# Hash attention with a gated feed-forward layer: two more transposes of x handed to DMA, and means, hashes, loads and sends in other slots

## The chip, the cores and the metric

The kernel runs on one core of a Trainium2 chip. A core has five engines that run side by side, each through its own stream of instructions, in order: TensorE (PE; PEld in the profile is its loading of weights), VectorE (DVE), ScalarE (ACT), GpSimd (POOL) and SyncE (SP), which here only starts DMAs. They meet through semaphores. DMAs are started by SP, by POOL or by ACT, and 16 DMA engines carry them. The metric is the device time of one execution in microseconds; the median of three runs of the kernel before is 327.64 us (327.44 to 327.68).

## The reference

```python
q_bits = (np.einsum('bhsd,dk->bhsk', q, proj) > 0)      # 6 bits for each row, as a bucket number
k_bits = (np.einsum('bhsd,dk->bhsk', k, proj) > 0)
mask   = q_bucket[:, :, :, None] == k_bucket[:, :, None, :]
scores = np.where(mask, scale * np.matmul(q, k.transpose(0, 1, 3, 2)), -1e9)
attn   = softmax(scores)                                # with 1e-9 added to the sum
x      = np.matmul(attn, v)                             # heads side by side: (3072, 512)
xn     = x / sqrt(mean(x * x) + 1e-6) * rms_g
out    = (silu(xn @ w_gate) * (xn @ w_val)) @ w_out
```

There are 4 batches of 8 heads, 768 rows, 64 columns for each head; the feed-forward layer is 512 to 1536 to 512. All inputs and the output are fp32.

## The kernel before

**Units and slots.** The work is cut into eight units: unit u is one half (384 rows) of batch u // 2. Unit u's attention goes head by head, and a head takes three slots; there are 192 slots in the main loop (line 889). In slot t, TensorE first gets the two score matmuls of slot t + 1 (`scores`, L349), ACT the exponential of slot t (`probs`, L361), and then everything that the list `plan[t]` holds, in order of insertion. The order of every engine's stream is thus written out by hand through `at(0, t, function, ...)`; nothing is reordered later. From unit 2 on, unit u's attention runs in slots 24u to 24u + 23. In the same slots stand the second half of the layer before: y = h w_out of unit u - 2 (`project`, L513, with a copy and a store to memory for each third), and then gate and value matmuls of unit u - 1 (`gate`, `value`, L484).

**The planner.** `spread` (L805 to L828) lays a window's `project` pieces and gate and value pieces over its slots by weight, so that each slot carries about as much as the others. At given slots it puts in extras: `hash_one` (weight 1000) and `v_mean` (weight 120). An entry `(HASH, None)` takes up the weight of a hash and does nothing; it stands where a pair's hash is done together with the next pair's (`WITH`, L780).

**A pair of heads** (b, hp) is heads 2hp and 2hp + 1 of batch b. Q, K and V are loaded by SP (`load_natural`, `load_v`, `load_blocks`) into eight buffers that rotate. Q and K are transposed, for the first six pairs on TensorE (`turn_pe`, L156), later on VectorE (`turn_dve`, L188 and L195), and cast by GpSimd (`cast_pool`) to rows 0 to 63 of one of six fp16 tiles `QK`. The hash is a matmul with the projection (`hash_direct` L238, `hash_one` L218); VectorE turns its signs into fp16 bit rows (L227), and small DMAs (`send_bits`, L308: eight for a pair, four for a head) put them into rows 64 to 69 of `QK`. The score matmul then adds a large constant for each equal bit, and the exponential's bias takes it away again: unequal buckets come out as zero.

**Means.** `v_mean` (L333) sums V's rows through a matmul with ones; times 1e-9 / 768 the sum is added to the numerator and denominator of attention (`cvb`, L336), for the reference's 1e-9. For batch 0's later pairs it reads the fp16 V (`parts`), otherwise GpSimd's partial sums (`v_sum`). Batch b's two means of four heads are extras at 5 and 18 slots into the batch.

**From attention to the layer.** `attn_out` (L388 to L404) adds cvb, takes the reciprocal on VectorE, and multiplies on GpSimd (or on VectorE, with `eng`), which gives x. The squares' sums go to `ssp`; `norm` (L446) forms 1/rms on GpSimd (L443) and xn on VectorE, in thirds of 128 rows. Each third must be transposed to xnT: either by TensorE (`turn_x`, L467) with a copy out of PSUM by VectorE (L473), or by a DMA that SP issues (`turn_dma`, L431). `ONDMA` (L426) says how many thirds of a unit go by DMA; those are scaled by `grow` in xn (L452), the others by `gcol` in the copy. A unit's first gate matmul needs all three. `norm` stands 4 slots into the window, `turn_dma` 5.

**PSUM.** Transposes, hashes, means, gates, values and y share three banks (`bank`).

Of the kernel before, what the change touches and what calls it, by code (L numbers as in the profile page):

```python
# [16 lines left out]
H = 8  # L17
S = 768
D = 64
DMODEL = H * D  # L20
# [13 lines left out]
def kernel(  # L34
# [12 lines left out]
    nc = tc.nc  # L47
# [40 lines left out]
    raw = {}  # L88

    def load_natural(eng, b, hp, which, heads=(0, 1)):  # L90
# [10 lines left out]
            ),  # L101
        )

    def load_v(eng, b, hp):
        vn = lpool.tile([128, 2, 6, D], FP32, name="vn", tag="L")
        eng.dma_start(
            out=vn.rearrange("p h c d -> p h (c d)"),
            in_=v[b, 2 * hp : 2 * hp + 2].rearrange("h (p c) d -> p h (c d)", c=6),
        )
        raw[b, hp][2] = vn  # L110

    def load_blocks(eng, b, hp):
        tiles = []
        for name, t in (("qL", q), ("kL", k)):
# [8 lines left out]
            tiles.append(lt)  # L123
        raw[b, hp] = tiles + [None]

# [173 lines left out]
        for n, pair in enumerate(pairs):  # L299
            hashed[pair] = where, bt, 12 * n  # L300

    def send_bits(b, hp, hh):

        where, bt, r = hashed[b, hp]
        for t, which, half in where:
            o = (0 if which == "q" else S) + half * HALF
            p0 = 32 * t + r + 6 * hh
            nc.sync.dma_start(  # L308
                out=QK[b, 2 * hp + hh, "h"][D:KROWS, o : o + HALF],
                in_=bt[p0 : p0 + 6, :],  # L310
            )
# [5 lines left out]
        eng.tensor_copy(vls[b % 2][:, hs, :, 0:64], vn)  # L317

    def v_sum(b, hp):
        vn = raw[b, hp][2]  # L320
# [4 lines left out]
        nc.gpsimd.tensor_add(vsum[b % 2][:, hs, 0:64], a[:, :, 0], a[:, :, 2])  # L325

    def v_mean(b, hp, n, parts=(None,)):

        hs = slice(2 * hp, 2 * hp + n)
        ps = bank("m_ps", [128, n, 65])  # L330
        for i, jt in enumerate(parts):
            rhs = vsum[b % 2][:, hs, 0:65] if jt is None else vls[b % 2][:, hs, jt, 0:65]
            nc.tensor.matmul(  # L333
                ps, ones16, rhs, start=(i == 0), stop=(i == len(parts) - 1)
            )
        nc.vector.tensor_scalar_mul(cvb[b % 2][:, hs, 0:65], ps, C0 / S)  # L336
# [44 lines left out]

    def attn_out(u, hp, eng=nc.gpsimd):
        b = u // 2
        if hp == 0:
# [38 lines left out]

    rstds = {}

    ONDMA = {2: 2, 3: 2, 4: 2, 5: 2, 6: 2, 7: 1}  # L426

    def turn_dma(u, c):
        if c == 0:
# [168 lines left out]
    def at(w, s, f, *a):  # L598
        plan[NS * w + s].append(lambda: f(*a))
# [70 lines left out]
    at(0, 1, load_natural, nc.sync, 0, 3, "q")  # L670
    at(0, 2, load_v, nc.sync, 0, 2)
    at(0, 2, load_v, nc.sync, 0, 3)
    at(0, 60, nc.sync.dma_start, grow, moe_rms_g.partition_broadcast(128))
    at(0, 65, nc.scalar.mul, grow, grow, float(DMODEL) ** 0.5)
    at(0, 6, v_prep, 0, 1)
    at(0, 15, v_prep, 0, 2)
    at(0, 19, v_prep, 0, 3, nc.vector)
    for hp, t in enumerate((6, 16, 21, 28)):
        at(0, t, v_mean, 0, hp, 2, *([range(6)] if hp else []))
    for i, (t, t2) in enumerate(((22, 25), (31, 31))):  # L680
        cols = slice(i * DFF // 2, (i + 1) * DFF // 2)
# [2 lines left out]
        at(0, 39 + 3 * i, load_w, wo, moe_w_out, 6 * i, 6)  # L684


    for hp, ts in ((0, (8, 22, 23, 24, 25, 24, 39, 26, 28, 42)), (1, (20, 27, 28, 29, 30, 29, 41, 32, 33, 43))):
        tl, ts = ts[0], ts[1:]
        for w in "kq":
            at(0, tl, load_natural, nc.sync, 1, hp, w)  # L690
        at(0, tl, load_v, nc.sync, 1, hp)
        at(0, ts[0], new_pair, 1, hp)
        for t, hh, w in zip(ts[0:4], (0, 1, 0, 1), "kkqq"):
            at(0, t, turn_pe, 1, hp, hh, w)
        at(0, ts[4], cast_pool, 1, hp, "k")
# [7 lines left out]
    spots = {  # L703
# [10 lines left out]
    }  # L714
    for i, t in ((0, 39), (1, 41), (2, 57), (3, 61)):
        at(0, t, zero_rows, i)
    TX = 37

    LAGS = (0, 0, 0, 0, 0, 1, 1)
    sqs = {}  # L720

    def o_step(u, hp, *eng):
# [11 lines left out]
    late = []  # L734
    for n, (u, h) in enumerate(order):
        t = 3 * n + 4 - ((u, h) == (0, H - 1))
        for part in range(2):
            at(0, t + part, av, u, h, part)
        if h % 2:
            if (u, h) == (0, H - 1):  # L740

                at(0, t + 1, o_step, u, h // 2, nc.vector)
                at(0, t + 1, norm_scale, u)
                at(0, t + 1, nc.vector.tensor_scalar_mul, gcol, gcol, float(DMODEL) ** 0.5)
                at(0, t + 2, hash_only, 1, 1)
                at(0, t + 2, hash_signs, 1, 1)
                at(0, t + 2, norm, u)
                at(0, TX-1, norm_third, u, 2, nc.scalar.mul)
                at(0, TX + 1, send_pair, 1, 1)
                for c in range(3):  # L750
                    at(0, TX, turn_x, u, c, c == 2)
                continue
            if (u, h) == order[-1]:
                at(0, t + 1, o_step, u, h // 2, nc.vector)
                continue

            steps = [(t + 1, o_step), (t + (3 if h == 7 else 4 if u == 7 else 6), s_step)]
# [24 lines left out]
        spot[3]: (HASH, hash_one, *WITH.get(pair, ()), pair) for pair, spot in spots.items()  # L782
    }
    for (pair,) in WITH.values():
        inserts[spots[pair][3]] = (HASH, None)
    for b in (1, 2, 3):
        for s, hp in ((5, 0), (18, 2)):
            assert 2 * b * NS + s not in inserts
            inserts[2 * b * NS + s] = (MEAN, v_mean, b, hp, 4)


    SENDS = {(2, 0, 0): 77, (2, 0, 1): 77, (2, 2, 1): 101, (3, 2, 1): 149}

    def place(t, step):
        if step[0] is None:
            return
        at(0, t, *step)
        if step[0] is hash_one:
            late.append((t, hash_bits, *step[1:]))
            for pair in step[1:]:  # L800
                for hh in range(2):
                    s = SENDS.get((*pair, hh), t)
                    late.append((max(s, t), send_bits, *pair, hh))

    def spread(t0, n, pieces):  # L805
        fixed = [SCORES + (AV if (t - 1) % 3 < 2 else 0) for t in range(t0, t0 + n)]
# [3 lines left out]
        for s in range(n):  # L810
            done += fixed[s]
            while i < len(pieces):
                weight, whole, steps = pieces[i]
                full = done + weight // 2 > total * (s + 1) // n
                if extra and whole and t0 + s >= extra[0][0] and (full or extra[0][1] > MEAN):
                    _, weight, *step = extra.pop(0)
                    place(t0 + s, step)
                    done += weight
                    continue
# [45 lines left out]
    def behind_norm(t):  # L865

        return t - t % NS + 9 if 1 <= t % NS < 9 else t

    for (b, hp), (load, kturns, qturns, _) in spots.items():
        at(0, load, load_blocks, nc.sync, b, hp)  # L870
        at(0, load, load_v, nc.sync, b, hp)
        at(0, min(kturns + qturns), new_pair, b, hp)
        for w, turns in (("k", kturns), ("q", qturns)):
# [74 lines left out]
```

## Time and profile before

| | us |
|---|---|
| median of three runs (lowest, highest) | 327.64 (327.44, 327.68) |
| the profiled execution, its own time | 326.68 |
| its span, from the first instruction to the last | 324.9 |
| ACT: 192 exponentials of 128x768 (L361) | 167.7 busy, 900 ns each |
| PE: scores, 384 matmuls of 128x384 (L349) | 93.5 busy |
| PE: gates and values, 768 matmuls of 128x384 (L484) | 82.7 + 81.8 busy |
| PE: transposes of x, 52 matmuls of 128x128 (L467) | 4.7 busy, 219 ns each |
| DVE: copies of those out of PSUM (L473) | 7.4 busy, 11 times |
| SP: DMA transposes of x (L431) | 11 issues |
| TensorE's granted clock | 0.999 |

The clock is granted in full all the time. A line of a timeline has the start in us, the length, the engine, the kernel's line, the operation, what it writes and reads, and the shape; "x4" is a run of four instructions, and a bracket names the idle time before it and what ended that. Consecutive matmuls overlap: the next one starts long before the one ahead has ended. Times of slots: TensorE begins slot 21 at 27.64, slot 54 at 73.91, slot 119 at 177.81 and slot 148 at 222.44.

### The profile page before, as it was taken

The numbers are of one execution on the slowest core, as the hardware profiler recorded it, in microseconds if no ns is written. First come the engines' busy times: TensorE is split into PE (matmuls) and PEld (weight loads), VectorE is DVE, ScalarE is ACT, GpSimd is POOL, SyncE is SP. The second block draws the span as 40 slices with busy tenths as digits, with TensorE's granted clock in tenths as the row PEclk, the third lists the DMA queues.
The fourth block names the chain that finished last, engine by engine and source line by source line (L and its number), as shares of the span: only waits on it lengthen the run. The fifth ranks groups of instructions, "written<-read, shape, count | busy, mean of one in ns | idle before, by whom it ended". The sixth has DMA issues, their size and how long they took to land.

```text
span 324.9 us, 7772 instructions
## 1 busy us (share of the span) xinstructions
PE 319.9 (98%) x2955; PEld 194.4 (60%) x2955; DVE 229.7 (71%) x512; ACT 228.4 (70%) x333; POOL 157.6 (49%) x204
## 2 busy tenths in 40 slices
PE   8999999999999999999999999999999999999996
PEld 3676666656566565655566565655666556665554
DVE  5887876859888568874888568785677536673870
ACT  7999887667688676776767776777777768744322
POOL 4999759955974363731883621752582111221000
PEclk9999999999999999999999999999999999999999
DMA  7942999988428864055547056002100030003002
GB/s 208 360 168 85 226 216 195 192 159 151 103 38 158 157 136 88 6 94 156 89 100 145 35 125 120 7 5 66 72 4 3 1 99 34 0 2 105 10 2 97
DMA packets 85741, 32.63 MB, mean 100 GB/s; under 512 B 70908, under 2 KB 82632, under 8 KB 85704
## 3 DMA queue, kind: packets, MB, share of 16 engines
q1 hardware_dynamic: 81800, 27.35, 36.1%
q0 software_dynamic: 3680, 4.72, 8.5%
q8 instruction: 23, 0.38, 0.5%
q14 instruction: 14, 0.11, 0.1%
q10 hardware_dynamic: 224, 0.07, 0.1%
HBM read 28.58 MB, written 6.29 MB: 107 GB/s over the span
## 4 chain that ended last, share of the span: by engine, by line
PE 98%; ACT 1%; DVE 0%; issue 0%
PE s_ps L349 20%; PE g_ps L484 19%; PE v_ps L484 19%; PE y_ps L513 18%; PE o_ps L374 11%; PE d_ps L218 2%; PE t_ps L156 2%; PE d_ps L238 2%; PE z_ps L580 1%; PE x_ps L467 1%; PE y_ps L532 1%; PE m_ps L333 1%; ACT psb L361 1%; DVE kT L158 0%; PE s_ps L156 0%
## 5 line engine op out<-in xcount | busy, mean ns | idle before, releaser
L361 ACT ACTIVATE psb<-s_ps,ebias 128x768 f16<-128x768 f32 x192 | 167.7, 900 | 20.0 <-PE s_ps L349 19.2
L349 PE MATMUL s_ps<-QK 128*128 128x384 f16 (+1 forms) x384 | 93.5, 326 | 1.2 <-ACT psb L361 1.1
L492 ACT ACTIVATE t<-g_ps 128x384 f32<-128x384 f32 x96 | 47.2, 492 | 52.2 <-PE g_ps L484 50.5
L484 PE MATMUL g_ps<-xnT,wg 128*128 128x384 f16 x384 | 82.7, 326 | 0.0
L484 PE MATMUL v_ps<-xnT,wv 128*128 128x384 f16 x384 | 81.8, 326 | 0.0
L501 DVE SCALAR_TENSOR_TENSOR a<-t,g_ps 128x384 f32<-128x384 f32 x96 | 53.0, 552 | 28.9 <-ACT t L492 27.2
L395 POOL TENSOR_TENSOR x<-otmp,rcp 128x384 f32<-128x384 f32 x30 | 25.1, 837 | 96.2 <-DVE rcp L393 95.8
L513 PE MATMUL y_ps<-wo,ht 128*128 128x512 f16 x276 | 67.7, 379 | 0.0
L502 DVE SCALAR_TENSOR_TENSOR ht<-a,v_ps 128x384 f16<-128x384 f32 x96 | 53.2, 554 | 11.5 <-PE v_ps L484 3.6
L374 PEld LDWEIGHTS <-psb 128*128 128x128 f16 x1152 | 51.9, 97 | 15.7 <-issue 1.2
L374 PE MATMUL o_ps<-vl,psb 128*128 128x65 f16 x1152 | 55.8, 193 | 0.0
L349 PEld LDWEIGHTS <-QK 128*128 128x128 f16 (+1 forms) x384 | 34.8, 98 | 33.7 <-issue 7.9
L484 PEld LDWEIGHTS <-wg 128*128 128x128 f16 x384 | 35.2, 97 | 21.2
L484 PEld LDWEIGHTS <-wv 128*128 128x128 f16 x384 | 35.1, 97 | 20.8 <-issue 0.2
L513 PEld LDWEIGHTS <-ht 128*128 128x128 f16 x276 | 24.9, 98 | 23.0
L525 ACT COPY ysb<-y_ps 128x512 f32<-128x512 f32 x23 | 13.5, 587 | 15.8 <-PE y_ps L513 15.8
L388 DVE TENSOR_TENSOR otmp<-o_ps,cvb 128x390 f32<-128x390 f32 x32 | 17.8, 557 | 7.1 <-PE o_ps L374 7.1
L208 POOL CAST QK<-qT 64x768 f16<-64x768 f32 x20 | 16.5, 823 | 10.3 <-DVE qT L195 9.5
L401 POOL TENSOR_TENSOR sq<-x 128x384 f32<-128x384 f32 x24 | 19.9, 828 | 1.9
L208 POOL CAST QK<-kT 64x768 f16<-64x768 f32 x20 | 16.4, 822 | 5.2 <-DVE kT L195 3.1
L473 DVE TENSOR_TENSOR xnT<-x_ps,gcol 128x512 f16<-128x512 f16 x11 | 7.4, 688 | 15.1 <-PE x_ps L467 15.0
L195 DVE STREAM_TRANSPOSE kT<-kL 128x192 f32<-128x192 f32 x32 | 16.4, 516 | 0.0
(85 smaller groups left out, 274.9 us busy)
## 6 DMA issues: line engine op xcount, KB each, us to landing
vn<-in_v_dram SPq DMA_DIRECT2D x16, 384.0 KB
out_dram<-ysb SPq DMA_DIRECT2D x23, 256.0 KB
qL<-in_q_dram SPq DMA_DIRECT2D x40, 96.0 KB
kL<-in_k_dram SPq DMA_DIRECT2D x40, 96.0 KB
kn<-in_k_dram SPq DMA_DIRECT2D x5, 384.0 KB
qn<-in_q_dram SPq DMA_DIRECT2D x5, 384.0 KB
wg<-in_moe_w_gate_dram POOLq DMA_DIRECT2D x2, 768.0 KB, 9.4
wv<-in_moe_w_val_dram POOLq DMA_DIRECT2D x2, 768.0 KB, 11.7
```

The source lines that it names most:

```text
L208: nc.gpsimd.tensor_copy(QK[b, 2 * hp + hh, "h"][0:64, o : o + S], src[64 * hh : 64 * hh + 64, :])
L349: nc.tensor.matmul(ps[:, j, 0:HALF], QK[b, h, "h"][rows, S + jt * 128 : S + (jt + 1) * 128], QK[b, h, "h"][rows, half * HALF : (half + 1) ...
L361: nc.scalar.activation(psb[u, h][:, 2 * ch : 2 * ch + 2, :], sps.pop((u, i))[:, :, 0:HALF], AF.Exp, bias=ebias, scale=ESCALE,)
L374: nc.tensor.matmul(o[:, c, hh, 0:65], psb[u, h][:, jt, c * 128 : (c + 1) * 128], vls[b % 2][:, h, 2 * (jt % 3) + jt // 3 if b in PARITY el ...
L388: nc.vector.tensor_add(tmp[:, :, :, 0:65], o[:, :, :, 0:65], cvb[b % 2][:, 2 * hp : 2 * hp + 2, 0:65].unsqueeze(1).to_broadcast([128, 3, 2 ...
L395: eng.tensor_mul(xd.rearrange("p c (h d) -> p c h d", h=2), tmp[:, :, :, 0:64], r.to_broadcast([128, 3, 2, 64]),)
L401: eng.tensor_mul(sq, xd, xd)
L484: nc.tensor.matmul(ps, w[:, kt, fs], xnT[u][:, kt, :], start=(kt == 0), stop=(kt == 3))
L492: nc.scalar.activation(t, fbank[u, ft, "g_ps"], AF.Tanh, scale=0.5)
L501: nc.vector.scalar_tensor_tensor(out=a, in0=t, scalar=1.0, in1=g, op0=ALU.add, op1=ALU.mult)
L502: nc.vector.scalar_tensor_tensor(out=ht[u][:, ft, :], in0=a, scalar=0.5, in1=vv, op0=ALU.mult, op1=ALU.mult)
L513: nc.tensor.matmul(y, ht[u][:, ft, c * 128 : (c + 1) * 128], wo[:, ft, :], start=(ft == 0), stop=(ft == NF - 1),)
```

## The change

The edits, by what they move:

1. `ONDMA`: unit 1's first two thirds go by DMA instead of TensorE (all three went by TensorE), unit 5's all three (two did). The load of `grow` moves from slot 60 to 3, its scaling on ACT from 65 to 49.
2. Unit 5's last pair is multiplied and squared on VectorE (`XDVE`).
3. The loads of pair (2, 0) move from slot 50 to 53 (K first, then Q) and 54 (V), behind unit 1's transposes in SP's order. Pair (1, 2)'s eight bit sends, on SP in slot 51, are issued by GpSimd in slot 54; its V work on GpSimd moves from 54 to 57. Two zeroings of `QK` tiles by GpSimd move from 57 and 61 to 66 and 69.
4. The hash of pair (1, 0) moves from slot 26 to 27, and the first transpose of K of pair (1, 1) from 27 to 26; that K is loaded in slot 17 instead of 20. The mean of pair (0, 3) moves from 28 to 21.
5. In `spread` an extra is put in at the first whole piece once it is a slot late, even where the slot isn't full, and the empty entry of pair (3, 0) is gone. By the planner's own arithmetic this moves pieces in slots 96 to 119 only: the means of batch 2 come in slots 101 and 114 (before: 103 and 119), gates and values up to four pieces later than before in the middle, and slot 119 now carries four of them where it had none. Unit 4 first uses the second mean in slot 116.
6. Five late V loads are two DMAs, one for each head (`VSPLIT`).
7. Two assertions: a mean is put in ahead of its use, and after its sums.

```diff
+    VSPLIT = {(2, 3), (3, 0), (3, 1), (3, 2), (3, 3)}
     def load_v(eng, b, hp):
-        eng.dma_start(
-            out=vn.rearrange("p h c d -> p h (c d)"),
+        for hs in (slice(0, 1), slice(1, 2)) if (b, hp) in VSPLIT else (slice(0, 2),):
+            eng.dma_start(
+                out=vn[:, hs].rearrange("p h c d -> p h (c d)"),
...
-    def send_bits(b, hp, hh):
+    def send_bits(b, hp, hh, eng=nc.sync):
-            nc.sync.dma_start(
+            eng.dma_start(
...
-    ONDMA = {2: 2, 3: 2, 4: 2, 5: 2, 6: 2, 7: 1}
+    ONDMA = {1: 2, 2: 2, 3: 2, 4: 2, 5: 3, 6: 2, 7: 1}
...
-    at(0, 60, nc.sync.dma_start, grow, moe_rms_g.partition_broadcast(128))
-    at(0, 65, nc.scalar.mul, grow, grow, float(DMODEL) ** 0.5)
+    at(0, 3, nc.sync.dma_start, grow, moe_rms_g.partition_broadcast(128))
+    at(0, 49, nc.scalar.mul, grow, grow, float(DMODEL) ** 0.5)
-    for hp, t in enumerate((6, 16, 21, 28)):
+    for hp, t in enumerate((6, 16, 21, 21)):
         at(0, t, v_mean, 0, hp, 2, *([range(6)] if hp else []))
-    for hp, ts in ((0, (8, 22, 23, 24, 25, 24, 39, 26, 28, 42)), (1, (20, 27, 28, 29, 30, 29, 41, 32, 33, 43))):
+    for hp, ts in ((0, (8, 22, 23, 24, 25, 24, 39, 27, 28, 42)), (1, (20, 26, 28, 29, 30, 29, 41, 32, 33, 43))):
-            at(0, tl, load_natural, nc.sync, 1, hp, w)
+            at(0, 17 if (hp, w) == (1, "k") else tl, load_natural, nc.sync, 1, hp, w)
...
-        (2, 0): (50, (63, 64, 65, 66), (67, 69, 70, 71), 73),
+        (2, 0): ((53, 53, 54), (63, 64, 65, 66), (67, 69, 70, 71), 73),
-    for i, t in ((0, 39), (1, 41), (2, 57), (3, 61)):
+    for i, t in ((0, 39), (1, 41), (2, 66), (3, 69)):
         at(0, t, zero_rows, i)
+    XDVE = (5,)
-            if (u, h) == order[-1]:
+            if (u, h) == order[-1] or u in XDVE and h == H - 1:
                 at(0, t + 1, o_step, u, h // 2, nc.vector)
...
     for (pair,) in WITH.values():
-        inserts[spots[pair][3]] = (HASH, None)
+        if pair == (2, 0):
+            inserts[spots[pair][3]] = (HASH, None)
+        else:
+            del inserts[spots[pair][3]]
-    SENDS = {(2, 0, 0): 77, (2, 0, 1): 77, (2, 2, 1): 101, (3, 2, 1): 149}
+    SENDS = {(1, 2, 0): 54, (1, 2, 1): 54, (2, 0, 0): 77, (2, 0, 1): 77, (2, 2, 1): 101, (3, 2, 1): 149}
+    ONPOOL = {(1, 2, 0), (1, 2, 1)}
...
-                if extra and whole and t0 + s >= extra[0][0] and (full or extra[0][1] > MEAN):
+                due = extra and t0 + s - extra[0][0]
+                if extra and whole and due >= 0 and (full or due or extra[0][1] > MEAN):
...
-        t = 54 if (b, hp) == (1, 2) else behind_norm(qturns[-1] + 2)
+        t = 57 if (b, hp) == (1, 2) else behind_norm(qturns[-1] + 2)
         at(0, t, v_prep, b, hp)
```

More of the change, by code (lines that the diff above doesn't have):

```diff
@@ L102, in load_natural, with load_blocks @@
         )
+    VSPLIT = {(2, 3), (3, 0), (3, 1), (3, 2), (3, 3)}
     def load_v(eng, b, hp):
         vn = lpool.tile([128, 2, 6, D], FP32, name="vn", tag="L")
-        eng.dma_start(
-            out=vn.rearrange("p h c d -> p h (c d)"),
-            in_=v[b, 2 * hp : 2 * hp + 2].rearrange("h (p c) d -> p h (c d)", c=6),
-        )
+        for hs in (slice(0, 1), slice(1, 2)) if (b, hp) in VSPLIT else (slice(0, 2),):
+            eng.dma_start(
+                out=vn[:, hs].rearrange("p h c d -> p h (c d)"),
+                in_=v[b, 2 * hp : 2 * hp + 2][hs].rearrange("h (p c) d -> p h (c d)", c=6),
+            )
         raw[b, hp][2] = vn
-    def load_blocks(eng, b, hp):
-        tiles = []
-        for name, t in (("qL", q), ("kL", k)):
+    def load_blocks(eng, b, hp, only=(0, 1)):
+        tiles = raw.setdefault((b, hp), [None] * 3)
+        for n in only:
+            name, t = (("qL", q), ("kL", k))[n]
             lt = lpool.tile([128, 24, 32], FP32, name=name, tag="L")
@@ L122, in load_blocks @@
                     )
-            tiles.append(lt)
-        raw[b, hp] = tiles + [None]
+            tiles[n] = lt
     PARITY = (0, 1)
@@ L319, in v_sum @@
     def v_sum(b, hp):
+        sums.add((b, hp))
         vn = raw[b, hp][2]
@@ L325, in v_sum @@
         nc.gpsimd.tensor_add(vsum[b % 2][:, hs, 0:64], a[:, :, 0], a[:, :, 2])
+    means, sums = set(), set()
     def v_mean(b, hp, n, parts=(None,)):
+        for p in range(hp, hp + n // 2):
+            assert parts != (None,) or (b, p) in sums
+            means.add((b, p))
         hs = slice(2 * hp, 2 * hp + n)
@@ L383, in attn_out @@
         b = u // 2
+        assert (b, hp) in means
         if hp == 0:
@@ L802, in place @@
                     s = SENDS.get((*pair, hh), t)
-                    late.append((max(s, t), send_bits, *pair, hh))
+                    eng = nc.gpsimd if (*pair, hh) in ONPOOL else nc.sync
+                    late.append((max(s, t), send_bits, *pair, hh, eng))
     def spread(t0, n, pieces):
@@ L869 @@
     for (b, hp), (load, kturns, qturns, _) in spots.items():
-        at(0, load, load_blocks, nc.sync, b, hp)
+        if type(load) is tuple:
+            for t, only in zip(load, ((1,), (0,))):
+                at(0, t, load_blocks, nc.sync, b, hp, only)
+            load = load[2]
+        else:
+            at(0, load, load_blocks, nc.sync, b, hp)
         at(0, load, load_v, nc.sync, b, hp)
```

## The prediction

> **What bounds the kernel.** I read the page's busy shares first, then its chain, then what TensorE waited for, then the timelines around the edited slots.
>
> ```profile
> PE 319.9 (98%) x2955; PEld 194.4 (60%) x2955; DVE 229.7 (71%) x512; ACT 228.4 (70%) x333; POOL 157.6 (49%) x204
> ...
> PE 98%; ACT 1%; DVE 0%; issue 0%
> ```
>
> TensorE is nearly the whole chain; the other engines have 29% or more to spare. So an edit pays by what it takes off TensorE's instruction stream, or by a short stall between two matmuls, and costs what TensorE then waits for. "Busy" counts a matmul until its modelled end and hides short stalls, so I go by starts: in the timeline the distance from one group's start to the next is what a group costs.
>
> The profiled execution took 326.68 us (span 324.9, 1.78 around it), 0.96 below the median 327.64. I work out a difference on the profiled execution and subtract it from the median.
>
> **Unit 1: two thirds of x by DMA.** TensorE before unit 1's first gate (start, length, group):
>
> ```profile
> 75.09 0.39 PE L467 MATMUL x_ps<-ident,xn 128*128 128x128 f16 x4
> 75.32 1.03 PE L513 MATMUL y_ps<-wo,ht 128*128 128x512 f16 x4
> ...
> 76.78 0.74 PE L467 MATMUL x_ps<-ident,xn 128*128 128x128 f16 x8
> 77.36 0.49 PE L349 MATMUL s_ps<-QK 128*128 128x384 f16 x2
> ...
> 78.82 0.49 PE L484 MATMUL g_ps<-xnT,wg 128*128 128x384 f16 x2
> ```
>
> Four transposes cost 75.32 - 75.09 = 0.23; the later eight 0.58, of which 0.12 is a wait for the first copy out of PSUM. Two thirds go, one (0.23) stays: 0.81 - 0.23 = **0.58 off the path**, and the first gate would start at 78.24. Bounds: 0.46 (the wait stays) to 0.58. The trace has a rule to weigh here. The row of these transposes has 219 ns each, but their starts are 0.23 / 4 = 56 ns apart, and the pitch is what the next matmul waits for. The Trainium skill, page "TensorE: Matmul & The Clock Gate", Part 4, gives about 275 ns for such a transpose in a kernel; by that figure the twelve of both units would be an estimated 3.3 us. The starts here speak against it as a price on the path.
>
> What the DMAs must meet:
>
> ```profile
> 72.47 0.88 POOL L443 TENSOR_TENSOR rstd<-ss,mhalf 128x3 f32<-128x3 f32 x1 [1.71 <-DVE ss L439]
> 73.39 2.76 DVE L460 TENSOR_SCALAR xn<-x,rstd 128x512 f16<-128x512 f32 x3 [1.00 <-POOL rstd L443]
> ```
>
> The two thirds now use the L452 form (750 ns; 1.41 for a pair): ready at about 74.14 and 74.81. They are issued by SP. For what an issue and its data take I use unit 5, the same two DMAs in a quiet stretch (last columns: DMA share, GB/s):
>
> ```profile
> 224.35 2.55 SPq L431 DMA_TRANSPOSE xnT<-xn  x2
> ```
> ```profile
> 227.50:228.00 0.50, 0.50 (x4) 0.26 (x3) 0.00 (x0) 0.50 (x1) 0.00 (x0) 1.00 0.13 23
> 228.00:228.50 0.50, 0.50 (x6) 0.25 (x5) 0.00 (x0) 0.09 (x1) 0.00 (x0) 1.00 0.03 9
> ```
>
> An issue holds SP 1.28 us, and the second one's data end before 228.0, at most 2.4 after its issue at 225.63. So in unit 1: issues at 74.2 and 75.5, data in by 77.9, the gate at 78.24: no wait, but only 0.3 to spare. Of the eleven issues the longest took 2021 ns; such a one would make the gate wait 0.4. The DMA engines moved at a share of 1.04 from 72 to 73 us; those are earlier loads, issued by 70.6. The loads of pair (2,0) that SP issued from 70.72 are now behind the transposes.
>
> **What queues behind that wait on SP**: eight block loads of (2,0) (3.46 + 2.65 = 6.1 us before), a store, its v. They end about 6 us later, at 83; data ended some 3 us after the last issue (77.04, traffic over at 80), so 86. VectorE turns these blocks first in slot 63, at 88.6. Price 0, bound 0 to 0.5; K goes first, which fits.
>
> **Unit 5: the last third by DMA, last x by VectorE.**
>
> ```profile
> 228.72 0.39 PE L467 MATMUL x_ps<-ident,xn 128*128 128x128 f16 x4
> 228.95 1.03 PE L513 MATMUL y_ps<-wo,ht 128*128 128x512 f16 x4
> ...
> 230.13 0.81 PE L484 MATMUL g_ps<-xnT,wg 128*128 128x384 f16 x4
> ```
>
> **0.23 goes**; the gate would start at 229.90. The third DMA is issued at 226.9, its data end by 229.3: 0.6 to spare. VectorE's chain to xn: the multiply on GpSimd (837 ns, with a hop) becomes one of 558 on VectorE, but a stream transpose of 0.5 that ran beside GpSimd now stands behind the squares: equal within 0.1. Four bit sends and two stores come 1.3 later on SP; the bits are for unit 6's head 5 (slot 158, 237 us). Bounds 0 to 0.23.
>
> **The early slots.** A mean that stood in a stall, and one in slot 28; and the stall after the mean of slot 119:
>
> ```profile
> 27.97 0.51 PE L333 MATMUL m_ps<-vl,ones 128*128 128x130 f16 x6
> 28.43 0.48 PE L349 MATMUL s_ps<-QK 70*128 70x384 f16 x2
> ...
> 178.40 0.28 PE L333 MATMUL m_ps<-vsum,ones 128*128 128x260 f16 x1
> 178.69 0.48 PE L349 MATMUL s_ps<-QK 128*128 128x384 f16 x2
> ```
>
> Six mean matmuls take 0.35 in slot 28 (34.45 to 34.80) but 0.46 in slot 21: 0.11 is a wait of the scores for ACT's exponentials. Pair 3's mean moved there fills it: **0.11**. Its vl is ready at 26.73 (VectorE's cast). The hash of pair (1,0) costs 31.88 to 33.18 = 1.30 with its scores, against 1.23 at 23.86; VectorE's last Q copy ended at 32.36, after the hash had begun. One slot later it doesn't: **0.07**. Its K of (1,1) is needed a slot earlier and loaded three slots earlier, behind transposes done at 23.1: covered. Both are bounded by 0 and themselves, since ACT (8.93 us busy of the ten from 20 to 30) can take the slack back.
>
> **The planner, slots 96 to 119 (unit 4's attention).** With no empty 1000-weight entry for (3,0), slots 96 to 119 carry even work, and batch 2's second mean moves from 119 to 114. In 119 the mean took 0.29 to the next scores, against 0.12 at 73.79: slot 119 was 0.88 long and ACT's exponential takes 0.90. **0.17** goes, bounds 0 to 0.17. The mean in 114 (PE at 171) needs sums that GpSimd ended at 166.1: no wait.
>
> **Parts at nothing.** grow's load in slot 3 adds 256 KB ahead of the bits of (0,1); about 0.9 us at the page's 290 GB/s, and the bits, issued by 17.0 on SP, are used at 20.9. Its 639 ns on ACT move to slot 49, beside 1.10 of idle at 68.39. Zeroing moves 2 x 2.65 of GpSimd time to 95 and 101, where it idles 1.74 and 3.36. Five split v loads add 5 x 0.6 on SP; the tightest is (3,0), ahead of four sends and unit 3's transposes (149.53 to 149.95, with TensorE's gate at 154.13 and data by 153.7). All bounds 0 to 0.3.
>
> **Bits of (1,2) by GpSimd.** No row has a small DMA from this queue. The bounds: SP's eight sends took 5.75, 0.66 to 0.93 each; GpSimd's own weight loads
>
> ```profile
> L585 POOL DMA_DIRECT2D wg<-in_moe_w_gate_dram x2: 806/906/1007, 30.3 to 38.5; - x2
> ```
>
> took up to 1.01, with 8.9 us or more to landing for 768 KB. GpSimd is free for them at 73.35. Head 4's four are issued by 77.4 at the latest, and the scores that read them stand at 82.34 - 0.58 = 81.76. With SP's kind of landing (last of four issued at 80.0, read without a stall at 82.34) they are early; with 8.9 us they would be 4.5 late. I take 0: 4.5 KB is nearer to SP's row than 768 KB is. GpSimd is held for at most 8.1 us, so x of unit 2 starts 1.4 later than 80.06, and pair (1,3)'s casts end near 89.9 instead of 88.05, for scores at 91.3: covered by 1.4.
>
> **Sum**: 0.58 + 0.23 + 0.11 + 0.07 + 0.17 = 1.16. 326.68 - 1.16 = 325.5 for the profiled execution, and 327.64 - 1.16 = **326.5** for the median.
>
> **The rivals.**
> - *A gate waits for its DMA transposes* (17%). For: 0.3 and 0.6 to spare, an issue of 2021 ns in the rows. Against: none of the other units' gates waits on one now. It returns 0.4 to 0.9: 326.9 to 327.4.
> - *GpSimd's queue is late* (9%): slower. If its small DMAs land more than 8.4 us after 73.35 for four of them (1.4 each and 2.8 to land, say), TensorE stands at head 4's scores, 1 us for each us; over 1.2 us of GpSimd per send, the casts of (1,3) are late too. From 1.2 us of lateness the kernel is slower; at the 4.5 above it is 331. The Trainium skill, page "SBUF — State Buffer", section "SBUF: two separate sides", says that VectorE in a two-port mode keeps GpSimd from writing descriptors, so that a DMA of 620 ns took 3100; by it four sends would be an estimated 12 us. Against: in that stretch VectorE has one short row of such a form (480 ns), among rows that read PSUM or two tensors.
> - *Only the transposes pay* (8%): the early and planner terms are taken back by ACT: 327.64 - 0.81 = 326.8.
> - *A transpose costs its duration* (2%): 12 x 219 ns = 2.6, with the rest 324.7. Pitch speaks against it.
> - *More than the sum* (4%): GpSimd's and VectorE's relief around 75 us closes other short stalls: 326.0.
>
> **How the numbers follow.** The forecast has 60%, 326.1 to 326.9. The range 325.9 to 327.8 takes in the waiting gates and the lesser sums, and leaves out the late queue and the duration rival. About 0.2% (0.65 us, to 326.98) is what a measurement can tell from no change. Faster: 60 + 4 + 2 and half of the 8: 70%; within: the other half and the waiting gates but 1, 20%; slower: the late queue, and 1 from a gate that waits longest, 10%.
>
> **What would show it.** TensorE's x_ps group at 40 instead of 52 matmuls; unit 1's first gate right behind its y_ps group; no stall of the scores after the mean near 28 and near slot 119; GpSimd's eight issues each under 1.0 us, and no wait at head 4's scores near 81. A DMA named as releaser of g_ps or s_ps would prove me wrong, as would a GpSimd send of over 1.2 us.

## The result, and the profile after

The changed kernel takes 328.03 us (median of 22 runs, 327.60 to 328.92) against 327.28 for the kernel before on the same chip (22 runs, 326.73 to 328.26). The ratio is 1.0024, with a 95% interval of 1.0016 to 1.0031: slower by some 0.75 us, where 1.16 us of gain was predicted. The profiled execution took 328.73 us, span 326.9. Of the runs below, one execution of e5_shift took 670 us and one of e8_before_shift 415 us; they are in no ratio.

The page of the changed kernel, busy shares and the chain that ended last:

```profile
PE 320.4 (98%) x2943; PEld 194.0 (59%) x2943; DVE 227.5 (70%) x510; ACT 228.4 (70%) x333; POOL 160.4 (49%) x211
...
PE 94%; DMA 2%; DVE 1%; ACT 1%; SPq 0%; issue 0%; POOL 0%
```

The twelve transposes are gone from TensorE (2955 to 2943 matmuls), but the chain now leaves TensorE: 2% of the span is time in which it runs through a DMA, from issue to landing. (In the changed kernel L359 are the scores, L495 gates and values, L442 the DMA transposes, L312 the bit sends.) Its TensorE timeline shows where (start, length, group, and in a bracket the idle time and its releaser). The four places are the means in slot 21, which now take 0.69 for twelve, and the first gates of units 1, 3 and 5:

```profile
29.00 0.85 PE L343 MATMUL m_ps<-vl,ones 128*128 128x130 f16 x12
29.69 0.49 PE L359 MATMUL s_ps<-QK 70*128 70x384 f16 x2
...
78.21 1.02 PE L524 MATMUL y_ps<-wo,ht 128*128 128x512 f16 x4
79.51 0.48 PE L495 MATMUL g_ps<-xnT,wg 128*128 128x384 f16 x2 [0.27 <-DMA xnT<-xn]
...
153.94 1.03 PE L524 MATMUL y_ps<-wo,ht 128*128 128x512 f16 x4
156.44 0.48 PE L495 MATMUL g_ps<-xnT,wg 128*128 128x384 f16 x2 [1.47 <-DMA xnT<-xn]
...
231.84 0.49 PE L359 MATMUL s_ps<-QK 128*128 128x384 f16 x2
232.17 0.65 PE L495 MATMUL g_ps<-xnT,wg 128*128 128x384 f16 x3
```

Four y matmuls cost 0.86 to 0.87 by starts where nothing waits. At unit 1 it is 79.51 - 78.21 = 1.30, a wait of 0.43; at unit 3 it is 2.50, a wait of 1.63. Unit 3's transposes were on DMA before too; there the gate did not wait. The kernel before:

```profile
153.53 0.49 PE L349 MATMUL s_ps<-QK 128*128 128x384 f16 x2
153.85 0.44 PE L374 MATMUL o_ps<-vl,psb 128*128 128x65 f16 x9
154.13 0.81 PE L484 MATMUL g_ps<-xnT,wg 128*128 128x384 f16 x4
```

To see what each part gave I take, slot by slot, the start of the scores in both profiles, and subtract:

| stretch | predicted | measured |
|---|---|---|
| start, up to the first scores | 0 | +1.06 |
| early slots (to slot 53) | -0.18 | -0.23 |
| unit 1's window | -0.58 | -0.14 |
| slots 96 to 121 (planner, unit 3's gate) | -0.17 | +1.56 |
| unit 5's window | -0.23 | -0.22 |

The start belongs to the execution, not to the change: over the profiles of this study the first scores come 0.1 to 1.2 us later than in the one of before, in repeats of one kernel as in others. Below, "the end" is the shift of the last scores with the start taken off: +0.97 here. The other two differences are the question: 0.44 missing at unit 1, and 1.7 lost at unit 3.

What SP did, in the changed kernel (start, time held, count):

```profile
75.00 2.63 SPq L442 DMA_TRANSPOSE xnT<-xn  x2
...
146.22 1.06 SPq L110 DMA_DIRECT2D vn<-in_v_dram  x2
147.38 3.03 SPq L312 DMA_DIRECT2D QK<-bits  x4
...
151.00 2.59 SPq L442 DMA_TRANSPOSE xnT<-xn  x2
```

and GpSimd beside unit 1's transposes:

```profile
74.15 4.09 POOL L312 DMA_DIRECT2D QK<-bits  x8
```

With the late start allowed for, unit 1's transposes were issued when predicted (75.00 and 76.42), but by the trace their data landed 3.2 and 2.95 us later, not 2.4. Eight sends by GpSimd, 0.51 us each, were in flight with them. Unit 3's were issued at 151.00 and 152.38; the first landed after 2.45, the second only after 3.9, at 156.30. There is one more DMA in that moment. The page's list of queues has this line:

```profile
q8 instruction: 23, 0.38, 0.5%
```

23 packets of 16 KB. By their number they are TensorE's own instructions: it has 2 x 2943 of them (a weight load and a matmul each), so one packet per 256; e5_shift and e8_before_shift below move them by changing nothing but TensorE's stream. Such a fetch, a single packet, ran at 153.35 for 1.48 us. Beside it some packets of the second transpose took 1.2 to 1.4 us each; in the kernel before none of its 256-byte packets took over 0.06. There the fetch came at 154.69, after both transposes had landed (152.00 and 153.30). But that trace has two other such meetings. The first transposes of units 2 and 6 were issued at 110.34 and 261.06, and fetches started 0.36 and 0.41 after them: SP was held 1.82 and 2.02 us instead of 1.20 to 1.27, and the data landed after 3.00 and 3.17 instead of 2.43 to 2.54. Those gates did not wait.

### The profile page after: what moved, and what is told of

It is laid out like the page before. It is cut to its first block, busy times and chain, and to the rows that moved or that the text cites. A ratio compares the mean times of both kernels' runs of the same rounds, so it can differ in the third digit from the quotient of the medians.

```text
span 326.9 us, 7765 instructions
## 1 busy us (share of the span) xinstructions
PE 320.4 (98%) x2943; PEld 194.0 (59%) x2943; DVE 227.5 (70%) x510; ACT 228.4 (70%) x333; POOL 160.4 (49%) x211
## 4 chain that ended last, share of the span: by engine, by line
PE 94%; DMA 2%; DVE 1%; ACT 1%; SPq 0%; issue 0%; POOL 0%
PE g_ps L495 19%; PE v_ps L495 19%; PE s_ps L359 19%; PE y_ps L524 16%; PE o_ps L384 10%; PE t_ps L160 2%; PE d_ps L222 2%; DMA xnT<-xn 2%; PE d_ps L242 2%; PE z_ps L591 1%; PE y_ps L543 1%; ACT psb L371 1%; PE x_ps L478 1%; PE m_ps L343 1%; SPq L442 0%; DVE xn L463 0%
## 5 line engine op out<-in xcount | busy, mean ns | idle before, releaser
L359 PE MATMUL s_ps<-QK 128*128 128x384 f16 (+1 forms) x384 | 93.5, 326 | 1.2 <-ACT psb L371 1.1
L495 PE MATMUL g_ps<-xnT,wg 128*128 128x384 f16 x384 | 82.5, 326 | 1.8 <-DMA xnT<-xn 1.7
L495 PE MATMUL v_ps<-xnT,wv 128*128 128x384 f16 x384 | 82.0, 326 | 0.0
L406 POOL TENSOR_TENSOR x<-otmp,rcp 128x384 f32<-128x384 f32 x29 | 24.3, 838 | 91.3 <-DVE rcp L404 91.1
L359 PEld LDWEIGHTS <-QK 128*128 128x128 f16 (+1 forms) x384 | 34.7, 98 | 33.8 <-issue 8.6
L495 PEld LDWEIGHTS <-wg 128*128 128x128 f16 x384 | 35.1, 97 | 23.5 <-issue 2.7
L495 PEld LDWEIGHTS <-wv 128*128 128x128 f16 x384 | 35.1, 97 | 20.8 <-issue 0.2
L199 DVE STREAM_TRANSPOSE qT<-qL 128x192 f32<-128x192 f32 x32 | 16.1, 523 | 0.0
```

The source lines that it names most:

```text
L199: nc.vector.transpose(dst.rearrange("p (c t r) -> p r c t", c=6, r=4)[:, r], src.rearrange("p (r c) d -> p r c d", r=4)[:, r],)
L359: nc.tensor.matmul(ps[:, j, 0:HALF], QK[b, h, "h"][rows, S + jt * 128 : S + (jt + 1) * 128], QK[b, h, "h"][rows, half * HALF : (half + 1) ...
L406: eng.tensor_mul(xd.rearrange("p c (h d) -> p c h d", h=2), tmp[:, :, :, 0:64], r.to_broadcast([128, 3, 2, 64]),)
L495: nc.tensor.matmul(ps, w[:, kt, fs], xnT[u][:, kt, :], start=(kt == 0), stop=(kt == 3))
```

## The experiments

Three theories. **A1**: unit 3's transposes are late because SP is (split v loads). **A2**: they are late because the planner's edit moves TensorE's fetch onto the second one. **B**: unit 1's are late because GpSimd's sends share the DMA engines with them. Times are medians; ratios, with their 95% intervals, are to runs of the kernel before on the same chip.

**e1_again**: the changed kernel, unedited.

> The changed kernel again, unaltered. In its first profile two gates waited: unit 1's for 0.43 us and unit 3's for 1.63, and the first scores came 1.06 late. Theory A (both waits belong to the order of the program): they are there again at the same size within 0.3, the late start is not. Rival (chance of one execution): unit 3's wait is gone or far smaller. Time 0.6 to 0.9 us above the kernel before.

327.88 us, ratio 1.0019 (1.0009 to 1.0028). The waits are 0.43 at unit 1 and 1.17 at unit 3, the start only +0.12, the end +0.51: both waits recur, unit 3's smaller by 0.46, which is more than the 0.3 that was expected.

**e2_nosplit**: no split v loads.

```diff
-    VSPLIT = {(2, 3), (3, 0), (3, 1), (3, 2), (3, 3)}
+    VSPLIT = set()
```

> The changed kernel with the five V loads whole again. SP was 0.48 us longer at V of (3, 0), and unit 3's first DMA transpose was issued at 151.00, right behind a store. Theory A1 (the split load makes the transposes late): they are issued 0.4 to 0.5 earlier against TensorE, and unit 3's gate waits 0.5 to 1.2 instead of 1.63, none of it if that is all; time 0.4 to 1.6 below the changed kernel. Rival A2 (the second transpose stood behind TensorE's instruction fetch of 16 KB, which took 1.5 us of one DMA engine at 153.35, and that fetch moved through the planner's edit): the wait stays at 1.0 or more.

327.85 us, 1.0016 (1.0005 to 1.0027). By TensorE's clock, SP issues unit 3's transposes 0.8 to 1.0 earlier than in the two profiles of the changed kernel, the second still lands 3.96 after its issue, and the wait is 0.59 in this profile. That wait lies in the range that A1 expected; the time does not, it is that of the changed kernel within the interval. So a late SP is not what makes the landing long, but how much it adds to the wait stays open.

**e3_noplan**: edit 5 taken back. As in the kernel before, batch 2's second mean then comes after its first use.

```diff
-        assert (b, hp) in means
...
-        if pair == (2, 0):
-            inserts[spots[pair][3]] = (HASH, None)
-        else:
-            del inserts[spots[pair][3]]
+        inserts[spots[pair][3]] = (HASH, None)
...
-                if extra and whole and due >= 0 and (full or due or extra[0][1] > MEAN):
+                if extra and whole and due >= 0 and (full or extra[0][1] > MEAN):
```

> The changed kernel with the planner as before (an extra waits for a full slot, the empty entry of (3, 0) is back), so slots 96 to 119 are those of the kernel before; batch 2's second mean comes after its first use again. Theory A2 (the planner's edit put the fetch of instructions on top of unit 3's second transpose): the gate waits 0.3 or less, slot 119's stall of 0.17 is back, time 1.2 to 1.5 below the changed kernel. Rival A1 (only SP's lateness counts): the gate still waits 1.0 or more, since the split load stays.

326.73 us, 0.9989 (0.9980 to 0.9997). The split loads and the late SP are still there, the fetch now runs at 155.54, the transposes land in 2.45 and 2.5, and unit 3's gate does not wait. With edit 5 the change is slower than the kernel before, without it slightly faster. The pieces that edit 5 moves could still be the cause; e5_shift keeps them.

**e4_nosends**: the eight sends on GpSimd's queue are left out, so heads 4 and 5 of batch 1 get no bits.

```diff
-                    late.append((max(s, t), send_bits, *pair, hh, eng))
+                    if (*pair, hh) not in ONPOOL:
+                        late.append((max(s, t), send_bits, *pair, hh, eng))
```

> The changed kernel without GpSimd's eight bit sends of pair (1, 2): they are left out, so heads 4 and 5 of batch 1 get no bits. Unit 1's transposes were issued at 75.00 and 76.42 as forecast (75.0 and 76.3 with the late start), but their data were in only 3.2 and 2.95 us later instead of 2.4. Theory B (the sends, in flight beside them on the same DMA engines, slow them): 2.3 to 2.5 us each, and unit 1's gate waits 0.1 or less instead of 0.43. Rival (another cause, such as the first use of a queue): the wait stays. Time at most 0.5 below the changed kernel.

327.63 us, 1.0011 (1.0002 to 1.0019). TensorE in this run:

```profile
77.63 1.02 PE L524 MATMUL y_ps<-wo,ht 128*128 128x512 f16 x4
78.49 0.49 PE L495 MATMUL g_ps<-xnT,wg 128*128 128x384 f16 x2
```

0.86 again, so no wait. The two transposes, issued at 74.42 and 75.84, landed after 2.55 and 2.43, and unit 1's step is -0.58, as predicted. B holds. Unit 3's gate still waits 1.47. The other runs agree: in the six profiles with all eight sends beside them (the changed kernel, e1, e2, e3, e5, e10) the first transpose takes 3.2 to 3.5 and the second, where there is one, 2.9; with four sends, all issued before the second (e9, e13), 3.1 to 3.5 and 2.4; with none (e4, e6, e7) 2.55 and 2.4.

**e5_shift**: a test of A2 that touches nothing near unit 3. The warm-up before the first hash becomes 36 matmuls of 85 columns instead of 6 of 512 (`idle` gets a width `w`): the same width in sum, 30 more pairs of weight load and matmul, so that every later 256th instruction falls elsewhere.

```diff
-    idle(6)
+    idle(36, w=85)
```

> The changed kernel, planner's edit and split loads kept; the six warm-up matmuls of 512 columns at the start, where TensorE waits for its first K anyway, are 36 of 85 columns. TensorE's stream gets 30 pairs of weight load and matmul longer there and nothing else changes; at some 9.5 pairs per us around 150 us every later fetch of 16 KB of its instructions comes some 3 us sooner, so the one at 153.35 should be over before unit 3's second transpose moves data. Theory A2 (the fetch holds that transpose up): unit 3's gate waits 0.4 or less instead of 1.2 to 1.6, time 0.8 to 1.4 below the changed kernel. Rival A1 (SP's lateness, or the moved pieces, make the wait): it stays at 1.0 or more.

326.93 us, 0.9991 (0.9981 to 1.0001): 0.95 to 1.1 us less than the changed kernel's two medians, by an edit of the warm-up. The fetch went to 148.3, and TensorE before unit 3's gate now reads:

```profile
153.09 1.03 PE L524 MATMUL y_ps<-wo,ht 128*128 128x512 f16 x4
153.96 0.49 PE L495 MATMUL g_ps<-xnT,wg 128*128 128x384 f16 x2
```

0.87: no wait. Unit 1's wait of 0.42 is as before. The end is -0.81. A2 holds: SP's queue and the moved pieces are as in the changed kernel.

**e8_before_shift**: the reverse, the kernel before with 20 more pairs.

```diff
-    idle(6)
+    idle(26, w=118)
```

> The kernel before, with 26 warm-up matmuls of 118 columns for the six of 512: 20 pairs more in TensorE's stream, nothing else. The fetch that came at 154.69, after unit 3's transposes had landed, should come about 2.1 us sooner, at 152.6, on the data of the second one. Theory A2: unit 3's gate, which waited for nothing, now waits 0.5 to 1.3, and the kernel before gets 0.4 to 1.3 slower by twenty small matmuls in an idle stretch. Rival: 0.2 or less.

327.53 us, 1.0011 (0.9999 to 1.0023). The fetch went 5.7 us ahead, to 149.0, where it met the first transpose (landed after 2.8) and not the second. No wait; no test.

**e6_sends** and **e7_both**: the sends moved out from beside unit 1's transposes, head 4's to SP behind them and head 5's to GpSimd in slot 56; e6 on e3_noplan, e7 on e5_shift.

```diff
-    SENDS = {(1, 2, 0): 54, (1, 2, 1): 54, ...
+    SENDS = {(1, 2, 0): 53, (1, 2, 1): 56, ...
-    ONPOOL = {(1, 2, 0), (1, 2, 1)}
+    ONPOOL = {(1, 2, 1)}
```

> As e3_noplan (planner as before), and the eight bit sends taken apart: head 4's four by SP behind unit 1's transposes (slot 53), head 5's four by GpSimd behind unit 2's first x (slot 56). Theory B (sends in flight beside the transposes slow them): nothing is in flight beside them, they take 2.3 to 2.5 us to land, unit 1's gate waits 0.1 or less; time 0.3 to 0.5 below e3_noplan, 0.7 to 1.0 below the kernel before. Rival: the wait of 0.43 stays, or the scores of head 4 (about 83) or VectorE's block transposes of (2, 0) (about 89) now wait, and the time is e3_noplan's or more.

> The changed kernel with both mendings: the sends as in e6_sends and the 30 pairs as in e5_shift, the planner's edit kept. If A2 and B are right and nothing else is, it has the whole gain that was forecast: 1.0 to 1.3 below the kernel before, the fastest of all. If a fetch now falls on another transpose that has less to spare, or slot 119's 0.17 was no gain, 0.5 to 0.9.

Both miss: 328.17 us, 1.0030 (1.0019 to 1.0041), and 328.28 us, 1.0033 (1.0020 to 1.0045). Unit 1's wait is gone in both (step -0.57 in e6), but there is a new one ahead of the scores of pair (1,3), 1.46 in e6 and 0.60 in e7 (whose profile is its fastest run of five, 327.52). In e6's TensorE timeline:

```profile
93.63 0.48 PE L359 MATMUL s_ps<-QK 128*128 128x384 f16 x2 [1.30 <-DMA QK<-bits]
```

SP's loads of (2,0) now end at 87.25 instead of 83.15, and the bits of (1,3) are sent from 89.05, behind them and behind a store that lands only at 93.24. The two sends that these scores need land 4.2 and 3.6 us after their issue; in e9 below it is 1.9 and 1.8.

**e9_pool56**: e5_shift, with only head 5's sends moved, on GpSimd, so that SP's queue stays as it is.

```diff
-    SENDS = {(1, 2, 0): 54, (1, 2, 1): 54, ...
+    SENDS = {(1, 2, 0): 54, (1, 2, 1): 56, ...
```

> The changed kernel with the warm-up of e5_shift (30 more weight-load and matmul pairs of the same summed width, so that TensorE's instruction fetch misses unit 3's transposes), and of the eight sends of pair (1,2)'s bits on GpSimd's queue the four of head 5 two slots later (slot 56). If the sends beside the transposes are what delays them, and if half of them is enough to delay the first transpose only: unit 1's gate waits 0 to 0.2 us (e5_shift: 0.43), GpSimd's casts of pair (1,3) end near 90 instead of 88 with no wait on TensorE, and the profile's end without its start lies 0.2 to 0.45 below e5_shift's. If four sends delay both transposes as eight did: 0.4 again and no gain. If the later casts of pair (1,3) are what made e6_sends wait at 92.0 us (and not SP's later queue): a wait of 0.5 to 1.5 us before the scores of pair (1,3).

326.46 us, 0.9973 (0.9963 to 0.9984): faster than both kernels. TensorE at unit 1's gate, and GpSimd, of this run:

```profile
78.34 1.03 PE L524 MATMUL y_ps<-wo,ht 128*128 128x512 f16 x4
79.20 0.49 PE L495 MATMUL g_ps<-xnT,wg 128*128 128x384 f16 x2
```

```profile
74.28 2.13 POOL L312 DMA_DIRECT2D QK<-bits  x4
...
81.86 2.03 POOL L312 DMA_DIRECT2D QK<-bits  x4
...
88.45 1.71 POOL L212 CAST QK<-qT 64x768 f16<-64x768 f32 x2
```

No wait, a step of -0.58; the transposes land after 3.1 and 2.4. The casts of (1,3) end at 90.16, as late as in e6 (90.22), and no scores wait: it wasn't the casts that made e6 late, and SP's queue is what differs. The end is -1.07.

**e10_third** and **e12_unit1**, both on e5_shift: unit 1 with one third by DMA, and unit 1 as in the kernel before (no DMA, bits by SP).

```diff
-    ONDMA = {1: 2, 2: 2, ...
+    ONDMA = {1: 1, 2: 2, ...      (e10)
+    ONDMA = {2: 2, ...            (e12, with ONPOOL empty and (1, 2) out of SENDS)
```

> The changed kernel with the warm-up of e5_shift, and unit 1 with one third by DMA instead of two; all eight sends stay on GpSimd's queue at slot 54. The transpose that landed last in the changed kernel (79.37 us) is not there; the first landed at 78.19 there. If the gate waited for the second alone: no wait, unit 1's step is -0.23 to -0.3 against the kernel before (changed kernel: -0.14), and the end without the start lies 0.05 to 0.15 below e5_shift's. If the first is late too once the gate comes earlier by nothing it waits for: the step is about -0.15 and the end the same as e5_shift's.

> The changed kernel with the warm-up of e5_shift and with unit 1 as in the kernel before: its three thirds on TensorE, and the bits of pair (1,2) sent by SP at their old slot. It leaves the early part, unit 5 and the planner's edit. If unit 1's part is worth what the profiles say (0.14 to 0.16 of its 0.58): the end without the start lies 0.15 above e5_shift's, the time between 326.9 and 327.2. If the sends on GpSimd's queue or the transposes cost something elsewhere that the steps do not show, e12_unit1 is as fast as e5_shift or faster; by e4_nosends a loss elsewhere is not expected.

e10: 326.79 us, 0.9979 (0.9969 to 0.9988), no wait, step -0.35. e12: 326.83 us, 0.9981 (0.9971 to 0.9992), step -0.13. The time is just below the range that was expected and can't be told from e5's. The step was not expected either: with all transposes on TensorE, the wait of 0.12 for the first copy out of PSUM is gone by something else in the change (which, was not tried). So in the changed kernel (-0.14) unit 1's two DMAs brought 0.01, and of the 0.58 that e4 and e9 have they bring 0.45.

**e11_onto, e14_onto7, e15_onto11**: the kernel before with 9, 7 and 11 more pairs in the warm-up, to put the fetch onto unit 3's transposes.

```diff
-    idle(6)
+    idle(15, w=205)      (e11; e14: 13 of 236; e15: 17 of 181)
```

> The kernel before, with its warm-up of 6 matmuls of 512 columns cut to 15 of 205 (9 more weight-load and matmul pairs, the same summed width); nothing of the change is in it. In e8_before_shift 20 more pairs moved TensorE's fetch near unit 3 from 154.69 to 149.0, 0.285 us per pair; 9 pairs should bring it to 152.1, which is 1.2 us after the second transpose's issue, where the changed kernel and its repeats had it 1.0 to 1.9 us after. If a fetch there is what delays that transpose: it lands 3.5 to 4 us after its issue instead of 2.4, unit 3's gate waits 0.3 to 1.0 us, and the kernel before becomes slower by about as much, with no part of the change. If the lateness of the changed kernel's SP queue is needed for the wait: landing near 153.3, no wait, same time.

> The kernel before with a warm-up of 13 matmuls of 236 columns: 7 more pairs, the fetch near unit 3 expected at 152.7 on the scale of before (0.8 to 1.8 us behind the second transpose's issue, depending on the execution). e11_onto (9 pairs) had the wait in its profile (0.73 us), but of its times only three of twelve (328.2 to 328.9) were that much longer, the others 327.1 to 327.6. If the fetch meets the transpose only in some executions: again a profile with a fetch between 152 and 153.2, and times in two groups, near 327.2 and near 328.3, with more of them in the upper one the closer the fetch is to 1.0 to 1.9 us behind the issue. If a fetch there were harmless: no wait and all times near 327.2.

> The kernel before with a warm-up of 17 matmuls of 181 columns: 11 more pairs, the fetch near unit 3 expected at 151.6 on the scale of before, 0.7 us behind the second transpose's issue. As for e14_onto7: by the theory of the fetch two groups of times with a share of long ones that the position sets (at the edge, few), by the rival none.

e11 hit. SP and TensorE of this run:

```profile
150.18 2.55 SPq L431 DMA_TRANSPOSE xnT<-xn  x2
```

```profile
154.50 0.44 PE L374 MATMUL o_ps<-vl,psb 128*128 128x65 f16 x9
155.67 0.81 PE L484 MATMUL g_ps<-xnT,wg 128*128 128x384 f16 x4 [0.74 <-DVE otmp L388]
```

From nine o matmuls to the gate it is 0.28 in the kernel before and 1.18 here: a wait of 0.90, with nothing of the change in the kernel. (VectorE's row is named as its releaser; the gate reads xnT, and the trace has the second transpose landing at 155.54.) The table sets the runs side by side: unit 3's transposes, the fetch next to them, and what the gate waits, in us.

| kernel | issued | landed | fetch, took | wait |
|---|---|---|---|---|
| before | 149.53, 150.87 | 152.00, 153.30 | 154.69, 1.33 | 0 |
| changed | 151.00, 152.38 | 153.45, 156.30 | 153.35, 1.48 | 1.63 |
| e1_again | 149.88, 151.24 | 152.33, 154.93 | 152.32, 1.16 | 1.17 |
| e2_nosplit | 149.72, 151.09 | 152.16, 155.05 | 152.94, 1.08 | 0.59 |
| e3_noplan | 150.31, 151.68 | 152.76, 154.18 | 155.54, 0.95 | 0 |
| e5_shift | 149.15, 150.66 | 151.78, 153.15 | 148.30, 1.20 | 0 |
| e11_onto | 150.18, 151.53 | 152.65, 155.54 | 152.50, 1.64 | 0.90 |
| e15_onto11 | 150.02, 151.37 | 153.56, 154.32 | 150.92, 1.10 | 0 |
| e14_onto7 | 150.26, 151.61 | 152.72, 154.03 | 155.42, 0.96 | 0 |

Wherever the fetch starts 1.0 to 1.9 us after the second issue, the second transpose lands 3.7 to 4.0 after it instead of 2.4 to 2.5; where it starts 0.9 after the first issue (e15), the first one lands 3.5 after it, and the second hides that. A DMA reports its landing in 16 signals. In e2's trace 15 of the second transpose's had come by 153.53 and the last came at 155.05, which fits one of the 16 DMA engines being held up. All transposes of the 17 profiles, 220 in number, say the same. The 26 with a fetch that starts 0.2 to 2.2 us after their issue land 3.0 to 4.4 after it. The 143 with no fetch from 2 us before to 2.5 after, and no send of GpSimd's beside them, land 2.4 to 2.6 after it, without exception. e14 missed: its fetch did not move ahead with the 7 pairs, as it did with 9, 11 and 20. The times of these three say less than the profiles: 327.51 us, 1.0008 (0.9996 to 1.0021), three of twelve runs at 328.2 to 328.9 and the others at 327.1 to 327.6; 327.48 us, 0.9999 (0.9979 to 1.0019); 327.37 us, 1.0001 (0.9988 to 1.0014). That e11's wait occurs in only some of its executions would fit, but a trace of a single execution can't show it; it stays open.

**e13_noplan56**: the changed kernel without edit 5 (the mean comes late again, as in e3), with e9's sends and the old warm-up.

```diff
-    SENDS = {(1, 2, 0): 54, (1, 2, 1): 54, ...
+    SENDS = {(1, 2, 0): 54, (1, 2, 1): 56, ...      (and the diff of e3_noplan)
```

> The changed kernel without edit 5 (the planner's rule and the empty entry of pair (3,0) as before, so that batch 2's second mean comes after its first use again, as in the kernel before), and with head 5's four sends on GpSimd's queue in slot 56; the warm-up is left alone. In e3_noplan the fetch near unit 3 stood at 155.54, behind the transposes; the sends add nothing to TensorE's stream, so it stays there. Expected: no wait at unit 3 and at unit 1, unit 1's step -0.58, slot 119's 0.17 not gained; 326.3 to 326.8, as fast as e9_pool56 within 0.2, without its warm-up edit. If e9_pool56's warm-up were a gain by itself (not only by the fetch): 0.3 or more behind it.

326.29 us, 0.9968 (0.9954 to 0.9982), step -0.57 at unit 1, fetch at 155.81, end -0.85. Unit 3's gate waits 0.19, which was not expected: the transposes take 2.5 each, but TensorE now comes earlier and the second lands at 154.48, when the gate would start at 154.42. That is what a late SP costs by itself. Beside e9 no difference that these intervals can tell: the warm-up is no gain by itself, a fetch elsewhere is.

## Why the prediction was wrong

Step by step, with what the runs put in its place:

- **What bounds the kernel, and a price by starts**: right. Unit 5's 0.23 measured 0.22. The early slots' 0.18 measured 0.23, though in e3 and e6 a short wait (0.21 at 29.9 us in e3) takes it back, and over the profiles it is 0.02 to 0.38, so this one depends on the execution.
- **Unit 1, work**: right in size, 0.58 (e4, e9), where the transposes land in time. Its 0.12 for the copy's wait is no gain of the DMAs, though: e12 has 0.13 with all transposes on TensorE.
- **Unit 1, landing**: the step that failed first. "data in by 77.9, the gate at 78.24: no wait, but only 0.3 to spare" took 2.4 us from unit 5, "the same two DMAs in a quiet stretch". But the same change put eight sends beside unit 1's; the data took 3.0 to 3.2 us, and 0.43 of the 0.58 went. (By their landing signals unit 5's two took 2.54 and 2.47; the half-microsecond windows from which the 2.4 was read hid a tenth.) The rival of a waiting gate foresaw the size of this wait, but for another reason, an issue that holds SP for 2021 ns. The Trainium skill, page "DMA: Bandwidth & Descriptors", section "Issuing engines are not separate DMA queues", says that DMAs started by SP, ACT or GpSimd run on the same 16 engines and interleave; e4 agrees (2.55 and 2.43 without the sends, 3.2 and 2.95 with).
- **Bits by GpSimd**: right at 0. Each issue took 0.51 us, the median landing 1.9 us, no scores waited. The range of 0 to 4.5 was too wide. The Trainium skill, page "DMA: Bandwidth & Descriptors", section "Anatomy of one DMA — SWDGE (gpsimd) path", fits 2.0 us plus bytes over 436e3, an estimated 2.0 for 4.5 KB; the row agrees with its 1.9. The rival by which VectorE keeps GpSimd from its descriptors did not show.
- **The planner's 0.17**: the mean now takes 0.11 in slot 114 instead of 0.29 in 119, but in the runs where unit 3's gate doesn't wait (e5, e9, e10, e12) the stretch gives only 0.05 to 0.07. In which slots the other 0.1 is lost stays open.
- **"All bounds 0 to 0.3" for unit 3's gate ("data by 153.7")**: the step that turned the sign. It compared an issue time plus a quiet landing with the gate, and counted SP's delay only. The planner's edit changes which instructions come ahead of slot 103, and so where a fetch falls; it fell on the second transpose, and the gate waited 1.2 to 1.6 us. The sign that the prediction named against itself, a DMA as releaser of g_ps, is there at both gates. The before trace could have raised the question: its fetch ran at 154.69, 1.4 us behind the landing, in a stretch whose instructions the change reorders. And it had already shown the price: the issue of 2021 ns, which the prediction took for a chance of SP's, is unit 6's at 261.06, the one beside a fetch.

Of the 1.16 us, 1.07 is there in e9's profile and some 0.9 (0.5 to 1.2) in its times, once the two DMA meetings are gone. But for them the sum was nearly right, and they cost 0.43 + 1.63 in the profile.

## What to carry to other kernels

A DMA's time from issue to landing holds only for the company it had in that row: list everything that the change itself puts in flight in the same two or three microseconds, on whatever queue, before subtracting. Where a matmul waits for a DMA with less than 2 us to spare (the longest landing here was 4.4 instead of 2.4), look up where the engine's instruction fetches fall; any edit ahead of it that adds, drops or reorders TensorE instructions moves them, and can cost or return more than the edit. Test such a suspicion by padding the warm-up, and keep a burst of small sends off the queue on which the next loads wait, and out of the moment in which a transpose is in flight.

## What the runs showed of the hardware

- TensorE's instructions come by DMA, 16 KB for 256 of them, 0.9 to 1.9 us each over the 17 profiles. A DMA transpose that meets such a fetch lands 3.0 to 4.4 us after its issue instead of 2.4 to 2.6; where the fetch starts within 0.75 us of the issue, SP is in most cases held longer too (up to 2.6 us instead of 1.2 to 1.3). The profile's page counts these fetches at 0.5% of the DMA engines' time, which hides that.
- Eight sends of 4.5 KB on GpSimd's queue lengthen two DMA transposes beside them from 2.4-2.6 to 2.9-3.5 us, though the DMA share of those stretches is only 0.32 and 0.50, and no smaller without the sends (0.72 and 0.41 in e4, where other loads run). So it is not the load that delays them; what in the two queues' meeting does, stays open.
- The fetch does not move in proportion to the instructions added: near unit 3, 0, 2.8, 4.3 and 5.8 us ahead on TensorE's clock for 7, 9, 11 and 20 more pairs (e14, e11, e15, e8). Why stays open.
